# Elementwise sums of a long convolution moved from VectorE to accumulating DMAs inside SBUF

## The chip, the cores and the metric

One core of a Trainium2 chip runs the whole kernel. TensorE (PE) multiplies matrices, ScalarE (ACT) brings its results out of PSUM and computes GELU and scalings, VectorE (DVE) does the elementwise work, GpSimd (POOL) and SyncE (SP) mostly issue DMAs. The metric is the device time of one execution in microseconds (us).

## The reference, cut to what matters

Two branches over the same input `x` (`A_q`, 2048 rows of 640) are mixed by a gate per row. Branch A is a short convolution, a product and a long convolution done by a Fourier transform; branch B is a mixer with two LayerNorms and an MLP.

```python
# A: short convolution of k with 4 taps, times v, then a long causal convolution
for t in range(ks):
    k_shift = k_shift + k_pad[:, t:t + S, :] * shift_k[:, ks - 1 - t][None, None, :]
kv = k_shift * v
y_f = rfft(pad(kv)) * rfft(pad(ssm_k))            # over 2*S points, per column
y = irfft(y_f)[:S] + kv * ssm_D
a = q * y
# B: mixer and MLP
h = gelu(layernorm(x) @ w1)                       # 640 -> 640
x1 = x + concat(four shifted quarters of h) @ w2
b = x1 + gelu(layernorm(x1) @ w3) @ w4            # 640 -> 1536 -> 640
out = g * a + (1 - g) * b                         # g = sigmoid((x * gate_w).sum(-1))
```

The order of the sums in the complex product and in the short convolution is free.

## The kernel before, in words

All data stay in one SBUF tensor, `arena`, 128 partitions wide; every tile is a stretch of it. So the profile names nearly every operand `arena`, and a helper's line stands for many operations: L453 is `tt`, every tensor-tensor operation of DVE; L480 is `evict`, every move from PSUM by ACT; L465 is `act`, ACT on SBUF data; L487 is `load`.

**Order of the work.** The kernel is first written down as a list of nodes in program order. Reads and writes are tracked in pieces of 32 bytes of a partition, and each node depends on the earlier nodes that touch its pieces. `schedule` (L140) then walks through time with an estimated cost for each node and gives every engine a fixed order: the node that can start first goes first, and among equals the one whose tag has the higher number in `PRIO` (L967). A tag is the operation's name and its stage, such as `pw:1`. The engines then run their lists in order, and wait on semaphores for what they need from others. A DMA is modelled as a queue common to all, 390 KB per us, plus 2 us.

**Branch B** runs in groups of rows. First LayerNorm (`ln_bn`, L632, statistics on DVE, the power on POOL at L646, normalization on ACT), transposes on PE (L620), the product with w1 (L715, 100 matmuls), GELU, small moves of the shifted tail from POOL's queue (L743), the product with w2 (L760, L762), second LayerNorm, then w3 (L792) and w4 (L808, L810). The tiles of w3 lie over w1 and w2, those of w4 over `kacc` and `ktmp`, so these loads wait until the earlier users are done. Q, the input once more for the end, lies over the transposed tile and is loaded after the last L792.

**Branch A** has these parts.
- The short convolution, tag `kv`, stages 0 to 3 (block c of 1024 rows, half h of it), L555 to L568: per stage four products of 2560 elements a partition, three sums into `kacc`, one product with v. All stages share one `kacc` and two `ktmp`.
- The long convolution splits the frequencies in two (`kap`) and the columns in two (`half`), so there are four units, run by `conv_unit` (L912) with stage 2*half + kap. Each unit has: `forward` (L834, PE at L844, 32 matmuls, once for the filter, tag `fwdh`, once for kv, `fwdk`), a `window` on the latter (2 operations of 1280), a `butterfly` on each (`bh`, `bk`; 2 operations of 2560, 4 of 1280), `pointwise` (L871, the complex products, 6 of 2560 and 8 of 1280) and `fold` (8 of 1280). The butterflies, the products and the fold all use the slot s4 as a temporary tile, so they follow one another.
- `inverse` (L923, PE at L934, 8 groups of 8 matmuls per half) brings two units back; its results are scaled by ACT (`gy`), multiplied by Q and added on DVE (`fin`), and stored.

At the end of the program `inverse` of the second half needs the fold of the fourth unit.

Of the kernel before, what the change touches and what calls it, by code (L numbers as in the profile page):

```python
# [10 lines left out]
ACTF = mybir.ActivationFunctionType  # L11
ALU = mybir.AluOpType
# [66 lines left out]
class Prog:  # L79
# [48 lines left out]
        job.pe = node  # L128
        return job

    def dma(self, queue, fn, r=(), w=(), nbytes=0, cost=0.1, kind="dma", group=None, final=False, tag=""):
        node = self._new(queue, [fn], cost, kind, r, w, group, tag)
        node.bytes = nbytes
        node.final = final
        return node

    RATE = 390e3
# [203 lines left out]
def bass_gated_mix__ssm_conv_h3__mixer_s_mlp__prompt_kernel(  # L341
# [5 lines left out]
    P = Prog(nc)  # L347
# [17 lines left out]
    def V(o, n):  # L365
        return AR[:, o:o + n]
# [31 lines left out]
    w1t = V(oW12 + 3200, 640).rearrange("p (c f) -> p c f", c=5)  # L398
# [3 lines left out]
    FM = V(oFM, 4096).rearrange("p (a r s i k) -> p a r s i k", a=2, r=4, s=2, i=2)  # L402
    GM = V(oGM, 4096).rearrange("p (a i r s k) -> p a i r s k", a=2, i=2, r=4, s=2)
    TAP = V(oTAP, 10240).rearrange("p (h t d) -> p h t d", h=2, t=16)
    KV = V(oKV, 10240).rearrange("p (t d) -> p t d", t=16)
    slots = {f"s{i}": oS + i * SLOT for i in range(5)}
# [3 lines left out]
    kacc = V(oW4, 2560).rearrange("p (r d) -> p r d", r=4)  # L410
# [41 lines left out]
    def tt(o, a, b, op, n, tag="", **kw):  # L452
        return dve(lambda e: e.tensor_tensor(o, a, b, op), [a, b], [o], n, tag=tag, **kw)  # L453
# [101 lines left out]
    for c in range(2):  # L555
        for h in range(2):
            P.stage = 2 * c + h
            for j in range(4):
                src = KH[c][:, 3 + 4 * h - j:7 + 4 * h - j, :]
                sb = SHK[:, j, :].unsqueeze(1).to_broadcast([128, 4, 640])  # L560
                if j == 0:
                    tt(kacc, src, sb, ALU.mult, 2560, tag="kv")
                else:
                    t = ktmp[j % 2]
                    tt(t, src, sb, ALU.mult, 2560, tag="kv")
                    tt(kacc, kacc, t, ALU.add, 2560, tag="kv")
            o = KV[:, 8 * c + 4 * h:8 * c + 4 * h + 4, :]
            tt(o, kacc, o, ALU.mult, 2560, tag="kv")  # L568

# [255 lines left out]
    def cplx(slot):  # L825

        if slot in ("k0", "k1"):
            return KV[:, :, 320 * int(slot[1]):320 * int(slot[1]) + 320]
        return V(slots[slot], SLOT).rearrange("p (n d) -> p n d", n=16)
# [35 lines left out]
    def window(slot, kap):  # L865
# [2 lines left out]
        tt(S[:, :, 0, 1, :], S[:, :, 0, 1, :], S[:, :, 1, 0, :], a, 1280, tag="win")  # L868
        tt(S[:, :, 1, 1, :], S[:, :, 1, 1, :], S[:, :, 0, 0, :], b, 1280, tag="win")

    def pointwise(sh, sk, sz, temp):  # L871
        H, K, Z = [cplx(s).rearrange("p (i m b) d -> p i m b d", i=2, m=4) for s in (sh, sk, sz)]
        T2 = [V(slots[temp] + 2560 * i, 2560).rearrange("p (m b d) -> p m b d", m=4, b=2) for i in range(2)]
        T1 = [V(slots[temp] + 1280 * i, 1280).rearrange("p (m d) -> p m d", m=4) for i in range(4)]

        def hb(i):
            return H[:, i, :, 0, :].unsqueeze(2).to_broadcast([128, 4, 2, 320])

        tt(Z[:, 0], K[:, 0], hb(0), ALU.mult, 2560, tag="pw")
        tt(T2[0], K[:, 1], hb(1), ALU.mult, 2560, tag="pw")  # L880
        tt(Z[:, 1], K[:, 1], hb(0), ALU.mult, 2560, tag="pw")
        tt(Z[:, 0], Z[:, 0], T2[0], ALU.subtract, 2560, tag="pw")
        tt(T2[1], K[:, 0], hb(1), ALU.mult, 2560, tag="pw")
        h1 = [H[:, i, :, 1, :] for i in range(2)]
        k0 = [K[:, i, :, 0, :] for i in range(2)]
        z1 = [Z[:, i, :, 1, :] for i in range(2)]
        tt(T1[0], k0[0], h1[0], ALU.mult, 1280, tag="pw")
        tt(T1[1], k0[1], h1[1], ALU.mult, 1280, tag="pw")
        tt(Z[:, 1], Z[:, 1], T2[1], ALU.add, 2560, tag="pw")
        tt(z1[0], z1[0], T1[0], ALU.add, 1280, tag="pw")  # L890
        tt(T1[2], k0[1], h1[0], ALU.mult, 1280, tag="pw")
        tt(z1[0], z1[0], T1[1], ALU.subtract, 1280, tag="pw")
        tt(T1[3], k0[0], h1[1], ALU.mult, 1280, tag="pw")
        tt(z1[1], z1[1], T1[2], ALU.add, 1280, tag="pw")
        tt(z1[1], z1[1], T1[3], ALU.add, 1280, tag="pw")
# [16 lines left out]
    def conv_unit(half, kap, A, B, C, T):  # L912
        P.stage = 2 * half + kap
        butterfly(A, T, "bh")
        forward("k", half, kap, B)
        window(B, kap)
        butterfly(B, T, "bk")
        pointwise(A, B, C, T)
        fold(C, T)

    gy_i = [0]
# [1 line left out]
    def inverse(half, slot0, slot1):  # L923
# [41 lines left out]
    inverse(1, "s3", "k0")  # L965

    P.PRIO = {  # L967
        "Sk:2": 147, "xn:4": 146, "fwdk:0": 145, "gelu1t:1": 144, "kv:2": 143, "B:1": 142, "B:0": 141,
        "bn:3": 140, "sq:6": 139, "bn:2": 138, "gelu3:0": 137, "w1t": 136, "mm1:0": 135, "ln:2": 134, "shk": 133,
        "B:3": 132, "warm": 131, "ln:6": 130, "xTp:3": 129, "inv:0": 128, "gate": 127, "bk:2": 126, "kv:3": 125,  # L970
        "tail:0": 124, "gy:0": 123, "Sh:1": 122, "tail:2": 121, "mm2:6": 120, "w2": 119, "xT:6": 118,
        "out:0": 117, "xT:4": 116, "xn:0": 115, "": 114, "w4": 113, "gelu1:3": 112, "gelu1:2": 111, "bk:1": 110,
        "x1:4": 109, "kh": 108, "fin:0": 107, "xTp:0": 106, "fold:1": 105, "tail:3": 104, "pw:3": 103,
        "bn:0": 102, "xn:3": 101, "win:1": 100, "fwdk:2": 99, "fold:2": 98, "bh:0": 97, "ln:4": 96, "mm4:3": 95,
        "mm2:4": 94, "kv:0": 93, "gelu3:2": 92, "q": 91, "Sk:1": 90, "xTe:3": 89, "B:2": 88, "gy:1": 87,
        "x1:6": 86, "pw:2": 85, "tap": 84, "mm4:2": 83, "xT:7": 82, "fwdh:3": 81, "bh:1": 80, "mm4:1": 79,
        "gelu1:1": 78, "fold:0": 77, "fold:3": 76, "mm1:3": 75, "pw:1": 74, "GM": 73, "mm3:0": 72, "Sh:0": 71,
        "x1:7": 70, "xn:1": 69, "drow": 68, "fwdh:1": 67, "x": 66, "Sh:2": 65, "out:1": 64, "mm1:2": 63,
        "fwdk:1": 62, "ln:3": 61, "gelu1:0": 60, "Sk:0": 59, "bk:0": 58, "xn:6": 57, "xTe:1": 56, "xTp:2": 55,
        "w1": 54, "k": 53, "Sk:3": 52, "fin:1": 51, "xT:5": 50, "win:3": 49, "kv:1": 48, "Sh:3": 47, "gw": 46,  # L980
        "ident": 45, "xTp:1": 44, "bh:2": 43, "fwdh:2": 42, "gsum": 41, "tail:1": 40, "xn:7": 39, "mm3:1": 38,
        "xTe:2": 37, "mm1:1": 36, "ln:0": 35, "pw:0": 34, "sq:7": 33, "v": 32, "gelu1t:0": 31, "xn:2": 30,
        "fwdh:0": 29, "w2t": 28, "ssm": 27, "ln:7": 26, "bn:1": 25, "bn:4": 24, "fwdk:3": 23, "inv:1": 22,
        "mm3:2": 21, "xTe:0": 20, "bn:5": 19, "gelu1t:2": 18, "ssmD": 17, "ln:5": 16, "mm3:3": 15, "x1:5": 14,
        "gelu3:3": 13, "w3": 12, "mm2:5": 11, "gelu3:1": 10, "win:2": 9, "bk:3": 8, "win:0": 7, "xn:5": 6,
        "ln:1": 5, "gelu1t:3": 4, "mm4:0": 4, "mm2:7": 3, "bh:3": 2, "FM": 1,
    }
    P.schedule()
    P.assign_waits()
# [30 lines left out]
```

## Time and profile before

| | us |
|---|---|
| median of 3 runs | 256.15 (254.56 to 256.36) |
| profiled execution | 255.79 |
| its span, first to last instruction | 253.7 |
| PE busy (1585 matmuls) | 227.5 |
| DVE busy (323 instructions) | 221.8 |
| ACT busy (244 instructions) | 166.9 |
| POOL busy (43 instructions) | 31.2 |
| granted TensorE clock, mean | 0.99 |

The span begins with the loads: the 16 DMA engines are busy through the first seven of the 40 slices, and move 27.81 MB in all. PE's matmuls are pipelined, so its busy time counts overlaps. One instruction of DVE begins some 0.07 us before the last one ends, so that a row of 1.485 us takes about 1.42 from start to start. In the instruction lists several instructions of one line are merged, and the first one's shape is printed for all.

### The profile page before, as it was taken

The numbers are of one execution on the slowest core, as the hardware profiler recorded it, in microseconds if no ns is written. First come the engines' busy times: TensorE is split into PE (matmuls) and PEld (weight loads), VectorE is DVE, ScalarE is ACT, GpSimd is POOL, SyncE is SP. The second block draws the span as 40 slices with busy tenths as digits, with TensorE's granted clock in tenths as the row PEclk, the third lists the DMA queues.
The fourth block names the chain that finished last, engine by engine and source line by source line (L and its number), as shares of the span: only waits on it lengthen the run. The fifth ranks groups of instructions, "written<-read, shape, count | busy, mean of one in ns | idle before, by whom it ended". The sixth has DMA issues, their size and how long they took to land.

```text
span 253.7 us, 3951 instructions
## 1 busy us (share of the span) xinstructions
PE 227.5 (90%) x1585; PEld 144.7 (57%) x1585; DVE 221.8 (87%) x323; ACT 166.9 (66%) x244; POOL 31.2 (12%) x43
## 2 busy tenths in 40 slices
PE   3037799999999999989999999999999999899992
PEld 1033446956677777634675476677545774377771
DVE  3959999999997999999299999999999999919084
ACT  6085899988699979954888867721744214417283
POOL 6114513006132030202100000000000000000000
PEclk9999999799999999999999999999999999999998
DMA  7999996001057003630056600000000000194034
GB/s 226 225 377 412 411 372 260 3 0 30 16 186 292 0 3 78 199 141 0 0 54 129 126 3 4 0 3 0 0 0 3 0 0 3 21 386 138 27 103 155
DMA packets 21666, 27.81 MB, mean 110 GB/s; under 512 B 12001, under 2 KB 17377, under 8 KB 21393
## 3 DMA queue, kind: packets, MB, share of 16 engines
q1 hardware_dynamic: 19520, 20.55, 25.6%
q0 software_dynamic: 1840, 5.71, 7.1%
q10 hardware_dynamic: 288, 1.31, 1.7%
q8 instruction: 12, 0.20, 0.3%
q14 instruction: 6, 0.04, 0.1%
HBM read 21.79 MB, written 2.62 MB: 96 GB/s over the span
## 4 chain that ended last, share of the span: by engine, by line
PE 80%; DMA 8%; ACT 8%; SPq 2%; issue 1%; DVE 0%; ACTq 0%
PE PS L808 21%; PE PS L792 20%; PE PS L844 12%; PE PS L760 9%; DMA arena<-in_B_w_dram 8%; PE PS L934 7%; PE PS L715 5%; ACT arena L480 5%; ACT arena L465 3%; SPq L487 2%; PE PS L578 2%; PE PS L762 2%; PE PS L810 2%; PE PS L673 1%; DVE arena L453 0%
## 5 line engine op out<-in xcount | busy, mean ns | idle before, releaser
L453 DVE TENSOR_TENSOR arena<-arena 128x1280 bf16<-128x1280 bf16 (+2 forms) x208 | 195.8, 999 | 19.9 <-ACT arena L480 12.8
L480 ACT ACTIVATE arena<-PS 128x640 bf16<-128x640 f32 (+3 forms) x129 | 96.4, 828 | 35.4 <-PE PS L792 24.2
L808 PE MATMUL PS<-arena 128*128 128x320 bf16 x384 | 56.7, 299 | 1.1 <-ACT arena L480 1.1
L792 PE MATMUL PS<-arena 128*128 128x512 bf16 x240 | 52.8, 379 | 1.8 <-DMA arena<-in_B_w_dram 1.8
L480 ACT ACTIVATE arena<-PS,arena 128x320 bf16<-128x320 f32 (+1 forms) x48 | 27.8, 613 | 39.2 <-PE PS L810 36.5
L808 PEld LDWEIGHTS PS<-arena 128*128 128x128 bf16 x384 | 37.4, 98 | 16.6 <-ACT arena L480 1.6
L792 PEld LDWEIGHTS PS<-arena 128*128 128x128 bf16 x240 | 23.4, 98 | 29.4 <-issue 2.1
L465 ACT ACTIVATE arena<-arena 128x640 bf16<-128x640 bf16 (+2 forms) x42 | 33.9, 853 | 6.6 <-DVE arena L647 5.8
L844 PE MATMUL PS<-arena 128*128 128x320 bf16 x256 | 36.2, 299 | 0.0
L844 PEld LDWEIGHTS PS<-arena 128*128 128x128 bf16 x256 | 25.0, 98 | 10.4
L715 PE MATMUL PS<-arena 128*128 128x512 bf16 x100 | 24.3, 396 | 5.7 <-DMA arena<-in_B_w_dram 3.2
L760 PE MATMUL PS<-arena 128*128 128x320 bf16 x160 | 26.2, 299 | 0.1
L640 DVE BATCH_NORM_STATS2 arena<-arena 128x6 f32<-128x320 bf16 x48 | 20.6, 471 | 3.2 <-DMA arena<-in_A_q_dram 3.1
L715 PEld LDWEIGHTS PS<-arena 128*128 128x128 bf16 x100 | 9.7, 101 | 17.7 <-DMA arena<-in_B_w_dram 3.5
L760 PEld LDWEIGHTS PS<-arena 128*128 128x128 bf16 x160 | 15.6, 98 | 6.3 <-issue 0.4
L934 PE MATMUL PS<-arena 128*128 128x320 bf16 x128 | 17.9, 299 | 0.0
L934 PEld LDWEIGHTS PS<-arena 128*128 128x128 bf16 x128 | 12.5, 98 | 5.0
L646 POOL TENSOR_TENSOR arena<-arena 128x4 f32<-128x4 f32 x6 | 9.4, 1566 | 32.3 <-DVE arena L645 32.3
L743 POOL DMA_DIRECT2D arena<-arena x18 | 9.5, 536 | 27.7 <-ACT arena L480 27.7
L620 PE MATMUL PS<-arena 128*128 128x128 bf16 x80 | 6.6, 242 | 4.5 <-ACT arena L465 4.5
L810 PE MATMUL PS<-arena 128*128 128x320 bf16 x32 | 9.6, 299 | 0.0
L762 PE MATMUL PS<-arena 128*128 128x320 bf16 x32 | 9.6, 299 | 0.0
(46 smaller groups left out, 71.3 us busy)
## 6 DMA issues: line engine op xcount, KB each, us to landing
arena<-in_A_q_dram SPq DMA_DIRECT2D x6, 640.0 KB, 7.1
arena<-in_B_w_dram POOLq DMA_DIRECT2D x4, 960.0 KB, 7.0
arena<-in_A_k_dram SPq DMA_DIRECT2D x4, 640.0 KB, 14.5
arena<-in_A_v_dram SPq DMA_DIRECT2D x4, 640.0 KB, 15.1
arena<-in_A_ssm_k_dram SPq DMA_DIRECT2D x5, 512.0 KB, 18.9
out_dram<-arena SPq DMA_DIRECT2D x16, 160.0 KB, 2.0
arena<-in_A_q_dram ACTq DMA_DIRECT2D x2, 640.0 KB, 5.6
arena<-cF SPq DMA_DIRECT2D x1, 1024.0 KB, 20.9
```

The lines of the kernel that those rows point to most:

```text
L453: return dve(lambda e: e.tensor_tensor(o, a, b, op), [a, b], [o], n, tag=tag, **kw)
L465: node = P.op("act", lambda e, ps: e.activation(o, i, func, **kw), r=r, w=[o], cost=c_act(n, naps, acc is not None), tag=tag, group=group)
L480: node = P.op("act", lambda e, ps: e.activation(ov, inner(ps), func, **kw), r=r, w=[o], cost=c_act(n, len(r), acc is not None), job=job, t ...
L640: dve(lambda e, o=o, x=x: e.bn_stats(o, x), [x], [o], 640, tag="bn", group=("bn", g, i))
L715: fns.append(lambda e, ps, b=b, c=c, lhsT=lhsT, sc=sc: e.matmul(bank(ps, b, 512), lhsT, XT[:, c, 2 * sc:2 * sc + 2, :], start=(c == 0), st ...
L760: fns.append(lambda e, ps, hh=hh, ft=ft, lhsT=lhsT: e.matmul(bank(ps, hh, 320), lhsT, w2v[:, ft, 320 * hh:320 * hh + 320], start=(ft == 0) ...
L762: fns.append(lambda e, ps, hh=hh, c=c, rho=rho: e.matmul(bank(ps, hh, 320), ident, X[:, c, rho, 320 * hh:320 * hh + 320], start=False, sto ...
L792: fns.append(lambda e, ps, b=b, ft=ft, c=c, sc=sc: e.matmul(bank(ps, b, 512), w3v[:, c, 128 * ft:128 * ft + 128], XT[:, c, 2 * sc:2 * sc + ...
L808: fns.append(lambda e, ps, hh=hh, ft=ft, lhsT=lhsT: e.matmul(bank(ps, hh, 320), lhsT, w4v[:, ft, 320 * hh:320 * hh + 320], start=(ft == 0) ...
L810: fns.append(lambda e, ps, hh=hh, c=c, rho=rho: e.matmul(bank(ps, hh, 320), ident, X[:, c, rho, 320 * hh:320 * hh + 320], start=False, sto ...
L844: fns.append(lambda e, ps, r=r, ri=ri, s=s, b=b, rhs=rhs: e.matmul(bank(ps, b, 320), FM[:, kap, r, s, ri, :], rhs, start=(s == 0), stop=(s ...
L934: fns.append(lambda e, ps, kap=kap, ri=ri, c=c, r=r, s=s, n=n: e.matmul(bank(ps, c, 320), GM[:, kap, ri, r, s, :], Qs[kap][:, r, ri, c, :] ...
```

## The change

- In the stages 2 and 3 of the short convolution (the second block), each of the three sums into `kacc` is a DMA that POOL issues, from `ktmp` into `kacc`, with addition at the destination. The first block keeps DVE's sums.
- In the units 0, 1 and 2, `pointwise_dma` takes the place of `pointwise`. It has 4 products of 2560 and 4 of 1280 on DVE, most of them written over one of their operands, a negation of 2560 elements on ACT, and six accumulating DMAs: two of 1280 elements a partition into the temporary tile (`pwa`), two of 2560 into the result (`pwb`), two of 1280 from the temporary tile into half of the result (`pwc`). Unit 3 keeps `pointwise`.
- In the planner's terms each such DMA holds POOL for 0.9 us and moves twice its bytes.
- Every number of `PRIO` is another, so the order on every engine and queue may be another too. Some of the new numbers, loads on SP: x 146, w1 128, k 105, v 85, w2 73 (before: x 66, w1 54, k 53, v 32, w2 119).

```diff
@@ kv @@
                     t = ktmp[j % 2]
                     tt(t, src, sb, ALU.mult, 2560, tag="kv")
-                    tt(kacc, kacc, t, ALU.add, 2560, tag="kv")
+                    if c == 0:
+                        tt(kacc, kacc, t, ALU.add, 2560, tag="kv")
+                    else:
+                        o, i = [a.rearrange("p (x r) d -> p x (r d)", x=2) for a in (kacc, t)]
+                        P.dma("pool", lambda e, ps, o=o, i=i: e.dma_start(o, i, accum_op=ALU.add, max_dma_last_dim=2560), r=[o, i], w=[o],
+                              nbytes=2 * 256 * 2560, cost=0.9, tag="kva")
...
+    def accumulate(o, i, n, tag):
+
+        P.dma("pool", lambda e, ps: e.dma_start(o, i, accum_op=ALU.add, max_dma_last_dim=2560), r=[o, i], w=[o], nbytes=2 * 256 * n, cost=0.9,
+              tag=tag)
+
+    def pointwise_dma(sh, sk, sz, temp):
+
+        H, K, Z = [cplx(s).rearrange("p (i m b) d -> p i m b d", i=2, m=4) for s in (sh, sk, sz)]
+        T1 = [V(slots[temp] + 1280 * i, 1280).rearrange("p (m d) -> p m d", m=4) for i in range(2)]
+        h1 = [H[:, i, :, 1, :] for i in range(2)]
+        k0 = [K[:, i, :, 0, :] for i in range(2)]
+        z1 = [Z[:, i, :, 1, :] for i in range(2)]
...
+        tt(T1[0], k0[0], h1[1], ALU.mult, 1280, tag="pw")
+        tt(T1[1], k0[0], h1[0], ALU.mult, 1280, tag="pw")
+        tt(Z[:, 0], K[:, 0], hb(0), ALU.mult, 2560, tag="pw")
+        tt(K[:, 0], K[:, 0], hb(1), ALU.mult, 2560, tag="pw")
+        act(H[:, 1], H[:, 1], ACTF.Copy, 2560, scale=-1.0, tag="neg")
+        tt(h1[0], k0[1], h1[0], ALU.mult, 1280, tag="pw")
+        tt(h1[1], k0[1], h1[1], ALU.mult, 1280, tag="pw")
+        accumulate(T1[0], h1[0], 1280, "pwa")
+        accumulate(T1[1], h1[1], 1280, "pwa")
+        tt(Z[:, 1], K[:, 1], hb(0), ALU.mult, 2560, tag="pw")
+        tt(K[:, 1], K[:, 1], hb(1), ALU.mult, 2560, tag="pw")
+        accumulate(rows(Z[:, 1]), rows(K[:, 0]), 2560, "pwb")
+        accumulate(rows(Z[:, 0]), rows(K[:, 1]), 2560, "pwb")
+        accumulate(z1[1], T1[0], 1280, "pwc")
+        accumulate(z1[0], T1[1], 1280, "pwc")
...
-        pointwise(A, B, C, T)
+        (pointwise if (half, kap) == (1, 1) else pointwise_dma)(A, B, C, T)
```

`hb(i)` is H's first half of part i, repeated over two blocks; `rows` is another view of the same bytes.

## The prediction

> **What bounds the kernel now.** I read the 40 slices first, then each engine's instructions in order of time, then the chain that ended last, the shapes of DVE's groups, and the DMA landings. From the slices (one digit is 6.34 us):
>
> ```profile
> PE   3037799999999999989999999999999999899992
> ...
> DVE  3959999999997999999299999999999999919084
> ACT  6085899988699979954888867721744214417283
> ```
>
> PE and DVE are both full from about 45 us on, ACT only up to about 64 us. Which of the two sets the end is seen in the instruction lists (start, length, what, idle before in brackets). PE:
>
> ```profile
> 20.55 6.92 PE L715 MATMUL PS<-arena 128*128 128x512 bf16 x25 [3.22 <-DMA arena<-in_B_w_dram]
> ...
> 77.14 4.51 PE L844 MATMUL PS<-arena 128*128 128x320 bf16 x32
> ...
> 239.80 8.86 PE L934 MATMUL PS<-arena 128*128 128x320 bf16 x64
> ```
>
> and DVE:
>
> ```profile
> 54.53 20.77 DVE L453 TENSOR_TENSOR arena<-arena 128x2560 bf16<-128x2560 bf16 x15
> ...
> 126.85 95.38 DVE L453 TENSOR_TENSOR arena<-arena 128x1280 bf16<-128x1280 bf16 x102 [3.85 <-ACT arena L480]
> 227.76 6.71 DVE L453 TENSOR_TENSOR arena<-arena 128x640 bf16<-128x640 bf16 x15 [5.53 <-DMA arena<-in_A_q_dram]
> ```
>
> DVE's frequency work is over at 126.85 + 95.38 = 222.2. The last inverse transform, which needs it, starts on PE only at 239.8, because PE still has L808 to do. So the convolution chain on DVE has 17.6 us of slack, and **PE is the bound**: the chain of waits is 80% PE, and PE's only idle after 20.5 us is 1.90 + 0.62 + 0.28 (on ACT, before 46 us), 1.81 (w3) and 1.11, 5.7 us in all. DVE time taken away is worth nothing by itself; a DVE chain made longer costs nothing up to 17.6 us and all beyond.
>
> **What is removed.** Rows by shape:
>
> ```profile
> L453 DVE TENSOR_TENSOR arena<-arena 128x2560 bf16<-128x2560 bf16 x72 | 103.9, 1485 | 0.4
> L453 DVE TENSOR_TENSOR arena<-arena 128x1280 bf16<-128x1280 bf16 x104 | 78.9, 819 | 5.9 <-ACT arena L480 5.6
> ```
>
> A pointwise of 6 x 1.485 + 8 x 0.819 = 15.5 becomes 4 x 1.485 + 4 x 0.819 = 9.2 us; three units, 18.7 us. Six kv sums go, 6 x 1.485 = 8.9. DVE loses 27.6 of 221.8 us. In place of it: three ACT negations of 2560. ACT's 1280-wide row is 1.257 and its 640-wide 0.733, so 0.82 ns an element and 2.3 us each (2.0 to 2.5); ACT has room after 100 us (51 of 95 us busy from 127 to 222). And 24 DMAs on POOL's queue: 12 of 655 KB, 12 of 328 KB.
>
> **One accumulating DMA.** No row shows one. The nearest are the moves inside SBUF that POOL issues at L743:
>
> ```profile
> arena<-arena POOLq DMA_DIRECT2D x6, 32.0 KB, 1.8
> ...
> arena<-in_B_w_dram POOLq DMA_DIRECT2D x2, 960.0 KB, 7.0
> ```
>
> (first line: between 45 and 70 us, DMA nearly idle; the same six between 20 and 45 us, DMA full, took 5.4.) The second line is the two w3 loads together; while they moved, slices showed 353 to 435 GB/s, say 380. They hold POOL 0.86 us each against 0.54 at L743, so the fixed part is 1.8 + 0.3 = 2.1 us. On top of it come the bytes at 380 GB/s: if only the addend counts, 1.72 us for 655 KB; if both operands are read over one path, 3.45; if the write shares it as well, 5.17. So d (655 KB) is 3.8, 5.55 or 7.3 us and c (328 KB) 2.95, 3.8 or 4.7. I take between the last two, d = 6.4 and c = 4.25, because half of these DMAs move runs of 640 bytes, and the tail row shows that company triples a landing.
>
> The Trainium skill, "DMA: Bandwidth & Descriptors", section "Anatomy of one DMA", gives 2.0 us plus bytes over 436 GB/s; "Collectives: The Full Stack", section "The bandwidth ceiling", says that an add costs two source reads and nothing more. By both, estimates are 5.0 and 3.5 us, and the forecast's sum would end PE-bound, at the first rival's time. Against the change speaks "SBUF — State Buffer", section "Summary": descriptor generation for POOL's DMAs starves while DVE runs in its 2x mode. The trace disagrees: DVE was busy 5.90 of 6.00 us from 58 to 64 us while the 1.8 us row landed.
>
> **kv, second block.** kacc is one buffer, so the three sums of a stage, and both stages, are serial: kv:2 from 48.1 us in before. A stage is two products, 3d, then one product. With 1.43 us from start to start, the two stages cost 7 products on the path (10 us with semaphores) and 6d, where before they ended at 73.4 (w4's load, which waits for them, goes out at 73.46), 25.3 us. Now 10 + 6 x 6.4 = 48.4. DVE waits there; butterfly bh:0 (5.8 us) moves in, so that is not lost.
>
> **A unit.** Before, a unit is 5.83 + 5.83 (butterflies) + 14.5 + 6.0 (fold) by start-to-start times, with window 1.5. After, 8.66 + a gap G in place of 14.5. The temp slot s4 serves both butterflies, the products and the fold of every unit, so the next butterfly can't fill G. pwb needs the last product, pwc needs pwb, fold needs pwc: G = d + c + 1 (two transfers side by side at each step; the part of the fold that needs only the first pair is taken off). At my values 11.7 us, against 5.8 of DVE saved in the unit.
>
> **The sum.** The head first. w1, x, k and v stand ahead of the four w2 loads on SP's queue now (priorities 128, 146, 105, 85 against 73; w2 was 119, w1 54, x 66). Those are 655 KB, 1.8 us at 370 GB/s, 2.9 at the 225 GB/s of the first 12 us. PE waited 3.2 us for w1 until 20.5; its XT is evicted at 18.6; ACT idles 2.97 us at 18.6 as DVE's LN steps stand behind the late x. I take 3 us earlier (0 to 3.5). So kv:2 starts at 45.1, kv ends at 45.1 + 48.4 = 93.5. Forward, eviction: 5.5 (77.31 to 82.85). Units: window 1.5, bk 5.83, 8.66, G, fold 6.0 = 22 + G; twice 26.3 + G (their windows fit in the gap); the last 32.2: 106.8 + 3 x 11.65 = 141.75. That is 240.75. I add 1 us a unit for the negation (the product h1[1] and the K1 product stand behind it on DVE, PSUM evictions of PE behind it on ACT) and 2 for the second LayerNorm's DVE work (16 x 0.471 + 8 x 0.198 = 9.1 us, most of it in the gaps): 245.75. The inverse can start 2 before that, when r = 0 is folded, 243.8; 8.71 of PE and the 5.0 us from PE's end (248.71) to 253.7 give a span of 257.5. The profiled time was 255.79 for a span of 253.7, so 259.6; the median of the runs shown stands 0.36 above it: **260.0**.
>
> PE meanwhile: mm2, fwdh:1 and fwdk:0 last it until about 92 to 96, when kv ends, so no gap is priced. POOL's queue is in order: w3, w4, GM and the LN powers (1.57 us) queue behind accumulates that wait for DVE; w3 late would be PE idle, in the range only.
>
> **The rivals.**
> 1. *Faster: DMA cheap, PE still the bound.* From 170.4 + 9d + 3c + 5 - 2 at or below 236.8 (PE's old 239.8 less 3), that is 9d + 3c up to 63.4, d about 5.8. Then only the head counts: 253.7 - 3 + 2.1 = 252.8, 253.1 at the median. For it: reading both operands gives 61.4, just inside. Against: my d leaves nothing for two DMAs meeting loads.
> 2. *Cover without gain.* The same, but the head's 3 us don't come: ACT is busy 22.8 of 24 us from 21 to 45 and may bound it. 255 to 257.
> 3. *Slow accumulates.* d = 7.3, c = 4.7: 250.2 + 5 - 2 + 8.7 + 5 = 266.9, 269 in time; with rows of 640 bytes slower still, beyond. Every stall then reaches PE too, since PE, ACT and POOL run in a fixed order.
>
> **How the numbers follow.** Forecast 0.35, rival 1 0.27, rival 2 0.20, rival 3 0.18. The low end 250.5 is rival 1 with two thirds of PE's later waits gone (2.6 us); the high end 269.5 takes in the upper bound of d and leaves out slower DMAs. One per cent, 2.6 us, is about what a measurement can tell: faster (under 253.6) 0.27, slower (over 258.7) 0.49, which is rival 3 and 0.31 of the forecast's spread; within 0.24, rival 2 and the rest of it.
>
> **What would show it.** Landings of the accumulates near 6.4 and 4.25 us; DVE busy about 194 us; DVE gaps near 12 us before three of the four folds; kv's last product near 93; mm1 starting near 18; PE waiting on DVE before the last L934. Wrong if d is under 5.8, if other DVE work fills the gaps, or if the head stays at 20.5.

## The result, and the profile after

The changed kernel takes 287.82 us (median of four runs, 284.29 to 289.98) against 256.25 for the kernel before on the same chip: 1.120 times as long, interval 1.109 to 1.132. The run of 289.98 is of a slower state and is left out of the ratio. The forecast was 260.0 with a range up to 269.5. The sign was right, the size was not. The profiled execution took 284.29 for a span of 282.2.

From the page of the changed kernel, the slices (7.06 us each) and the chain that ended last, by engine and by line:

```profile
PE   3039959988999299979698999999989999995491
...
DVE  4599998446893209932599940299970199999994
...
PEclk9999999999999779999799999999999999999688
...
DVE 36%; DMA 28%; PE 19%; ACT 10%; issue 4%; POOL 1%; ACTq 0%; POOLq 0%; DVEq 0%
DVE arena L454 33%; DMA arena<-arena 24%; PE PS L798 6%; ACT arena L481 6%; ACT arena L466 4%; PE PS L975 4%; DMA arena<-in_A_q_dram 3%; PE PS L850 3%; PE PS L721 3%; DVE arena L646 2%; PE PS L814 2%; POOL arena L879 1%; PE PS L679 1%; PE PS L626 1%; POOL arena L652 1%
```

Before, the chain was 80% PE. Now PE has 19% of it, and DVE and the DMAs have 64%, 24 of it in moves inside SBUF. Counted from 0, DVE has holes at the slices 7 to 9 and 12 to 14 (kv's second block and its end) and around 17, 24 and 30 (the three units). PE has holes too, at 13, 36 and 37, and its granted clock falls there or right after.

PE's instruction list of the changed kernel (start, length, what, idle before in brackets), where it waits longest after the head:

```profile
21.31 3.69 PE L721 MATMUL PS<-arena 128*128 128x512 bf16 x10 [1.42 <-ACT arena L481]
...
98.30 15.50 PE L850 MATMUL PS<-arena 128*128 128x320 bf16 x92 [5.32 <-DVE arena L454]
...
253.51 4.51 PE L975 MATMUL PS<-arena 128*128 128x320 bf16 x32
264.77 11.43 PE L975 MATMUL PS<-arena 128*128 128x320 bf16 x64 [6.75 <-DVE arena L454]
```

The product with w1 starts 0.8 us later than before, not earlier. PE runs out of other work twice: for 5.32 us until the second block of kv is there, and for 6.75 us until the last fold.

DVE's list shows the gaps, here of the units 1 and 2:

```profile
163.78 2.35 DVE L454 TENSOR_TENSOR arena<-arena 128x1280 bf16<-128x1280 bf16 x2 [0.59 <-ACT arena L466]
178.84 0.82 DVE L454 TENSOR_TENSOR arena<-arena 128x1280 bf16<-128x1280 bf16 x1 [12.71 <-DMA arena<-arena]
182.37 27.37 DVE L454 TENSOR_TENSOR arena<-arena 128x1280 bf16<-128x1280 bf16 x29 [2.70 <-DMA arena<-arena]
222.72 0.82 DVE L454 TENSOR_TENSOR arena<-arena 128x1280 bf16<-128x1280 bf16 x1 [12.97 <-DMA arena<-arena]
226.05 52.25 DVE L454 TENSOR_TENSOR arena<-arena 128x1280 bf16<-128x1280 bf16 x73 [2.50 <-DMA arena<-arena]
```

The last products of unit 1 end at 166.13; one operation of the fold can go at 178.84, the others from 182.37. Unit 2 has the same picture from 209.74 to 226.05. The landings behind it, from the page's DMA issues:

```profile
arena<-arena POOLq DMA_DIRECT2D x12, 640.0 KB, 7.0
...
arena<-arena POOLq DMA_DIRECT2D x12, 320.0 KB, 6.4
```

and pieces of the chain in order of time, from the end of kv and the ends of the units 1 and 2 (start, length, what):

```profile
89.49 7.07 DMA arena<-arena
96.66 1.50 DVE arena L454
98.30 4.44 PE PS L850 x16
...
166.54 10.45 DMA arena<-arena
177.70 4.65 DMA arena<-arena
...
210.15 10.59 DMA arena<-arena
221.41 4.61 DMA arena<-arena
```

One sum of 640 KB with no other sum beside it (kva, at 89.49) takes 7.07, the six of them 5.6 to 7.1 with a median of 6.4, as forecast. The second `pwb` of a unit, of the same size, takes 8.5 in unit 0 and 10.5 and 10.6 in the units 1 and 2. It isn't alone: POOL's list of unit 1 (issues only),

```profile
159.96 1.32 POOL L879 DMA_DIRECT2D arena<-arena  x1 [5.36 <-DVE arena L454]
162.75 1.18 POOL L879 DMA_DIRECT2D arena<-arena  x1 [1.47 <-DVE arena L454]
164.91 1.28 POOL L879 DMA_DIRECT2D arena<-arena  x1 [0.98 <-DVE arena L454]
166.54 1.20 POOL L879 DMA_DIRECT2D arena<-arena  x1 [0.34 <-DVE arena L454]
171.16 1.31 POOL L879 DMA_DIRECT2D arena<-arena  x1 [3.42 <-DMA arena<-arena]
177.70 1.28 POOL L879 DMA_DIRECT2D arena<-arena  x1 [5.24 <-DMA arena<-arena]
```

is one `pwa`, one `pwb`, the other `pwa`, the other `pwb` and the two `pwc`. They land after 5.8, 7.6, 7.6, 10.5, 7.7 and 4.6 us. So while the second `pwb` is under way (166.54 to 177.0), the first one flies until 170.4, the second `pwa` until 172.5 and the first `pwc` from 171.2. Only the last sum of the unit is alone again, and takes 4.6.

### The profile page after: what moved, and what is told of

Same layout as the page of the kernel before. It is cut to its first block, busy times and chain, and to the rows that moved or that the text cites. A ratio compares the mean times of both kernels' runs of the same rounds, so it can differ in the third digit from the quotient of the medians.

```text
span 282.2 us, 3966 instructions
## 1 busy us (share of the span) xinstructions
PE 235.3 (83%) x1585; PEld 143.1 (51%) x1585; DVE 195.9 (69%) x299; ACT 173.1 (61%) x247; POOL 60.8 (22%) x67
## 3 DMA queue, kind: packets, MB, share of 16 engines
HBM read 21.79 MB, written 2.62 MB: 87 GB/s over the span
## 4 chain that ended last, share of the span: by engine, by line
DVE 36%; DMA 28%; PE 19%; ACT 10%; issue 4%; POOL 1%; ACTq 0%; POOLq 0%; DVEq 0%
DVE arena L454 33%; DMA arena<-arena 24%; PE PS L798 6%; ACT arena L481 6%; ACT arena L466 4%; PE PS L975 4%; DMA arena<-in_A_q_dram 3%; PE PS L850 3%; PE PS L721 3%; DVE arena L646 2%; PE PS L814 2%; POOL arena L879 1%; PE PS L679 1%; PE PS L626 1%; POOL arena L652 1%
## 5 line engine op out<-in xcount | busy, mean ns | idle before, releaser
L454 DVE TENSOR_TENSOR arena<-arena 128x1280 bf16<-128x1280 bf16 (+2 forms) x184 | 170.0, 980 | 60.4 <-DMA arena<-arena 41.0
L481 ACT ACTIVATE arena<-PS,arena 128x320 bf16<-128x320 f32 (+1 forms) x48 | 27.8, 616 | 50.7 <-PE PS L816 38.8
L798 PE MATMUL PS<-arena 128*128 128x512 bf16 x240 | 54.8, 387 | 3.8 <-DMA arena<-arena 2.9
L814 PE MATMUL PS<-arena 128*128 128x320 bf16 x384 | 56.6, 299 | 1.2 <-ACT arena L481 1.2
L466 ACT ACTIVATE arena<-arena 128x640 bf16<-128x640 bf16 (+3 forms) x45 | 40.8, 957 | 13.4 <-DVE arena L454 5.2
L850 PE MATMUL PS<-arena 128*128 128x320 bf16 x256 | 39.9, 311 | 7.1 <-DVE arena L454 5.3
L879 POOL DMA_DIRECT2D arena<-arena x18 | 23.4, 1301 | 78.9 <-DVE arena L454 53.4
L766 PE MATMUL PS<-arena 128*128 128x320 bf16 x160 | 26.2, 299 | 2.0 <-DMA arena<-arena 2.0
L975 PE MATMUL PS<-arena 128*128 128x320 bf16 x128 | 20.6, 324 | 6.8 <-DVE arena L454 6.8
L721 PE MATMUL PS<-arena 128*128 128x512 bf16 x100 | 24.1, 396 | 2.4 <-ACT arena L481 2.4
L652 POOL TENSOR_TENSOR arena<-arena 128x4 f32<-128x4 f32 x6 | 8.6, 1433 | 21.6 <-DVE arena L651 18.7
L749 POOL DMA_DIRECT2D arena<-arena x18 | 10.1, 660 | 13.0 <-ACT arena L481 13.0
L571 POOL DMA_DIRECT2D arena<-arena x6 | 7.3, 1224 | 24.4 <-DMA arena<-arena 12.6
```

The costliest lines, as they stand in the source:

```text
L466: node = P.op("act", lambda e, ps: e.activation(o, i, func, **kw), r=r, w=[o], cost=c_act(n, naps, acc is not None), tag=tag, group=group)
L481: node = P.op("act", lambda e, ps: e.activation(ov, inner(ps), func, **kw), r=r, w=[o], cost=c_act(n, len(r), acc is not None), job=job, t ...
L652: P.op("pool", lambda e, ps: e.tensor_tensor(RS, VAR, HALF, ALU.pow), r=[VAR, HALF], w=[RS], cost=1.6, tag="ln")
L721: fns.append(lambda e, ps, b=b, c=c, lhsT=lhsT, sc=sc: e.matmul(bank(ps, b, 512), lhsT, XT[:, c, 2 * sc:2 * sc + 2, :], start=(c == 0), st ...
L766: fns.append(lambda e, ps, hh=hh, ft=ft, lhsT=lhsT: e.matmul(bank(ps, hh, 320), lhsT, w2v[:, ft, 320 * hh:320 * hh + 320], start=(ft == 0) ...
L798: fns.append(lambda e, ps, b=b, ft=ft, c=c, sc=sc: e.matmul(bank(ps, b, 512), w3v[:, c, 128 * ft:128 * ft + 128], XT[:, c, 2 * sc:2 * sc + ...
```

## The experiments

Theory after the first look: the bytes of the accumulates set the time, by holding up kv's second block and by gaps of 13 to 16 us in three units. Rivals: the new order alone is to blame; the fixed part of a DMA is; moving the bytes is, whether they are added or not; the planner believed the DMAs too cheap.

### The parts, with the planner choosing a new order

Sums on DVE again, with the new `PRIO` (e_order); only kv's sums by DMA (e_kv); only the products' (e_pw); no sums at all (e_none).

```diff
-                    if c == 0:
+                    if True:
                         tt(kacc, kacc, t, ALU.add, 2560, tag="kv")
...
-        (pointwise if (half, kap) == (1, 1) else pointwise_dma)(A, B, C, T)
+        pointwise(A, B, C, T)
```

Both edits are e_order, the second alone is e_kv, the first alone e_pw. In e_none `accumulate` and the accumulates of kv are taken out.

> All sums back on DVE as in the kernel before; only the new priority numbers, so the new order, stay. If the accumulating DMAs are the cause, this is a DVE chain that again ends with slack, and PE bounds: 253 to 259 us, DVE busy about 222. If the new order is the cause, most of the 31 us stays: over 275.

> Only kv's second block sums by DMA; pointwise as before. The chain theory: in the changed kernel the six serial landings (6.5 us each) make these two stages take 46 + 3 us from kv:2's first product, 25.3 before, so the chain is 22 to 24 us longer and spends the 17.6 us of slack: 258 to 264 us. If the loss sat in the products' sums alone: 253 to 257. If kv's part carried it all: over 275.

> Only the sums of three units' products by DMA; kv as before. The chain theory: a gap of 15 us (measured in the changed kernel) in place of 5.8 us of DVE work in each unit, 9 to 10 us a unit, 28 in all, less 17.6 of slack: 264 to 270 us. If kv's wait alone is the cause: 253 to 257. If the parts simply add up without slack in common: about 275.

> The 24 accumulating DMAs are left out and nothing takes their place, so the sums are missing from the result; products, negations and order rules stay. It shows what the idea is worth if the sums were free. PE-bound theory: DVE's 27.6 us are worth nothing but PE's stalls, 251 to 256 us. If DVE time were worth something by itself: under 245. If the order or the negations on ACT are the cause: over 270.

Measured, as ratios to the kernel before on the same chip: e_order 266.24 us (1.042, 1.038 to 1.046), e_kv 274.33 (1.076, 1.073 to 1.078), e_pw 322.69 (1.264, 1.261 to 1.267), e_none 268.83 (1.052, 1.049 to 1.056). None is where a theory put it, and e_none, which does less than e_order, is no faster. In all four the planner has drawn up another order, since it works on another list of nodes with the same numbers. In e_pw the order is so unlucky that PE stands idle for 51.81 us before the last inverse:

```profile
303.84 11.77 PE L975 MATMUL PS<-arena 128*128 128x320 bf16 x64 [51.81 <-DVE arena L454]
```

So these runs tell only one thing safely: without any accumulating DMA, an order drawn up with this `PRIO` still costs some 11 us (e_order). What a part costs can't be read from them; the order has to be held.

### The DMAs made small, or turned into copies

e_small sends only 64 elements a partition in each of the 24 DMAs; e_copy sends all bytes but doesn't add. Nodes and costs are the planner's same ones, and in e_copy every engine has the order of the changed kernel. In e_small it hasn't: the smaller DMAs touch fewer pieces, so the planner sees fewer dependencies, and from about 113 us on PE, ACT and DVE have a somewhat different order (PE, for one, 64 matmuls of `forward` in a row where the changed kernel has 32, then 10 of w3, then 32).

```diff
+        o, i = o[:, 0:1, 0:64], i[:, 0:1, 0:64]
```

(e_small, ahead of both kinds of DMA)

```diff
-        P.dma("pool", lambda e, ps: e.dma_start(o, i, accum_op=ALU.add, max_dma_last_dim=2560), r=[o, i], w=[o], nbytes=2 * 256 * n, cost=0.9,
+        P.dma("pool", lambda e, ps: e.dma_start(o, i, max_dma_last_dim=2560), r=[o, i], w=[o], nbytes=2 * 256 * n, cost=0.9,
```

(e_copy, likewise in kv)

> Every accumulating DMA stays with its waits but adds only the first 64 elements of each partition (16 KB instead of 655 or 328 KB), so most of each sum is left out of the result. If bytes make the landing long (7.0 and 6.4 us median in the changed kernel), it falls to 2 to 3 us, the chain is some 40 us shorter and PE bounds: 253 to 258 us. If the fixed part of such a DMA (issue 1.3 us, waits, POOL's order) makes it long, landings stay over 4 us and the time over 265.

> The same 24 DMAs with the same bytes, as plain copies: the sums are left out of the result, the addend overwrites the destination. If the second read of an add is what takes the time, 655 KB land in 2.1 + 1.7 to 3.5 = 4 to 5.5 us and the time falls to 256 to 268. If moving the bytes inside SBUF from POOL's queue is the price, add or not, landings stay at 6 to 7 us and the time over 278.

Measured: e_small 260.87 (1.020, 1.015 to 1.026), e_copy 264.73 (1.036, 1.031 to 1.040). In e_copy the landings are

```profile
arena<-arena POOLq DMA_DIRECT2D x12, 640.0 KB, 4.1
arena<-arena POOLq DMA_DIRECT2D x12, 320.0 KB, 3.6
```

and DVE's gap in unit 1 is half as long (its products end at 157.66):

```profile
164.87 0.82 DVE L454 TENSOR_TENSOR arena<-arena 128x1280 bf16<-128x1280 bf16 x1 [7.20 <-DMA arena<-arena]
165.85 25.11 DVE L454 TENSOR_TENSOR arena<-arena 128x1280 bf16<-128x1280 bf16 x27 [0.16 <-DMA arena<-arena]
```

In this unit the six land after 4.2, 3.8, 3.3, 4.1, 5.9 and 3.2 us, the second `pwb` after 4.1 where the sum needs 10.5. **The same bytes moved without adding cost 23 us less.** (Adding also cuts them into more packets: for one unit 2656 against 672. Whether a part of the 23 is due to that, no run separates.) The other 9 of the 32 us by which the changed kernel is slower are there with copies too; e_small, in its own order, has about 5.

How the 19.8 us between the spans of e_copy (262.4) and the changed kernel (282.2) reach PE is read from the two lists: in e_copy the last inverse, then 96 matmuls in a row, starts without a wait at 243.23,

```profile
243.23 13.20 PE L975 MATMUL PS<-arena 128*128 128x320 bf16 x96
```

in the changed kernel its first 32 matmuls start at 253.51. So 10.3 us arise in the middle, 6.75 as the wait before the last 64, and these take 11.43 for 8.8.

### Each half of the bytes

s_kv cuts only the products' DMAs to 64 elements a partition, s_pw only those of kv; the edit is the line of e_small at one place. s_pw has the changed kernel's order on every engine; s_kv, which its expectation says has it too, has the order of e_small.

> The changed kernel in exactly its order on every engine; kv's six accumulating DMAs whole, the 18 of the products with only the first 64 elements of each partition, so most of those sums is left out. With all 24 cut the time was 260.9, with none 287.8. Chain theory: the two parts share one slack; kv's bytes are worth 6 x 4.2 = 25 us on the chain and most of it goes into the slack: 262 to 270. If the parts add up without a slack: about 274. If kv's part is the cause alone: 283 to 288.

> As before in exactly the changed kernel's order, the 18 DMAs of the products whole, kv's six cut to 64 elements (most of those sums left out). Chain theory: three gaps of 15 us fall to some 6 when cut, so 27 us on the chain, most in the shared slack: 262 to 272. Additive without slack: about 274. If the products' part is the cause alone: 283 to 288.

Measured: s_kv 269.98 (1.057, 1.052 to 1.061), s_pw 278.02 (1.090, 1.086 to 1.095): 9.1 and 17.1 above e_small. kv's bytes can be priced twice, each time in one order: 9.1 us without the products' bytes (s_kv less e_small) and 9.8 with them (287.82 less s_pw). If the two parts shared a slack, the first would be smaller by it. So they share none to speak of, though s_kv's time alone lies inside the range that was expected from a shared one. The products' part, 17 to 18 us, was only measured together with the difference between the two orders. PE in s_kv, then in s_pw:

```profile
100.15 15.67 PE L850 MATMUL PS<-arena 128*128 128x320 bf16 x92 [5.05 <-DVE arena L454]
```

```profile
259.36 10.36 PE L976 MATMUL PS<-arena 128*128 128x320 bf16 x64 [7.75 <-DVE arena L454]
```

kv's lateness is paid at 100 us: PE has nothing else in its order then, and what is lost there is lost for good, though DVE still has slack at the end (in s_kv the last inverse starts at 247.52 without a wait). The products' lateness is paid partly in the units and partly before the last inverse.

### The order alone

p_dve keeps the exact order of the changed kernel, written out as a list, and puts a DVE sum where each DMA stood.

```diff
-    P.schedule()
+    P.replay(SEQ, PAIR)
```

> The changed kernel's order kept on every engine, but each of the 24 sums is a DVE operation at the place in the order where POOL issued the DMA; negations on ACT and products stay. If the DMAs' landings are the cause and the order in itself is sound, PE bounds again: 254 to 262 us. If the order is a cause of its own, it stays over 266 as with the new priorities and the old sums (266.2).

Measured: 265.04 (1.037, 1.033 to 1.041), between the two expectations and equal to e_copy. Sums on DVE in this order cost as much as copies by DMA. e_small stands 4.2 below; most of the difference is a fall of TensorE's clock near 40 us that the traces of p_dve and e_copy show and e_small's doesn't. The line of the clock on the pages of e_small and of p_dve (e_copy's reads like p_dve's), one fence each:

```profile
PEclk9999999999999999999999999999999999999998
```

```profile
PEclk9999995799999999999999999999999999999998
```

The product with w2 starts at 58.85 in e_small, at 62.35 in e_copy and 62.06 in p_dve. So the changed kernel's order costs 9 to 10 us with this fall; less the 3.2 to 3.5 us of it, some 6 are left, which is an estimate.

### The head

b_w2p holds the order of the kernel before and moves only w2's four loads, on SP's queue, from ahead of the others to behind the last of `ssm`; it tests the forecast's 3 us. b_ln, b_kh and b_khln hold the order of before as well: in b_ln the small steps of the first LayerNorm group go ahead of the second group's statistics; in b_kh the loads of `kh` go behind w1, with w2 first as before; b_khln is both. In each the edit is the list's.

> The kernel before with its order kept on every engine; only on SP's queue the four w2 loads (655 KB) are issued after the ssm loads and not ahead of kh, x and w1. The prediction's term for the head by itself: w1 and the second half of x land 1.8 to 2.9 us earlier, PE is bound from there on: 253 to 254.5 us against 256. If PE's start is set by something else (XT evicted at 18.6, LN steps on DVE, ACT): 255.5 to 257.

> The kernel before, order kept, but the small LayerNorm operations of group 1 stand on DVE ahead of group 2's statistics, which wait for the second half of x. ACT's wait of 2.97 us at 18.6 us should go. If ACT bounds the head (busy 22.8 of 24 us after it): 252.5 to 254.5. If PE's wait for w1 (until 20.5) bounds it: 255 to 256.5.

> The kernel before, order kept, but SP issues the halo loads kh (0.96 MB) after w1 and not ahead of x and w1; the w2 loads stay first. If what lands beside x's first half decides the head (in the new order, x's second half beside it, PE's first transposes came 2.6 us later; with kh beside it 2.0 later), then x's second half beside the end of the first half costs some of what w1's earlier landing gives: 254 to 257. If w1's landing alone decides: 252.5 to 254.

> Both of the last two edits. If the head is bound by ACT's start on group 1 and by w1 together, only this one gains all of it: 251.5 to 253.5. If x's first half lands later for it, no gain: 255 to 257.

Measured: b_w2p 257.12 (1.006, 1.004 to 1.009), b_ln 254.96 (0.9995, 0.9976 to 1.0015), b_kh 254.19 (0.998, 0.996 to 1.000), b_khln 254.08 (0.995, 0.993 to 0.997). In b_w2p w1 is early and PE's wait for it is gone, but the first transposes start later, since the first half of x, loaded over ACT's queue, lands later. The DMA issues of b_w2p and its PE list:

```profile
arena<-in_A_q_dram ACTq DMA_DIRECT2D x2, 640.0 KB, 6.5
```

```profile
16.55 1.23 PE L644 MATMUL PS<-arena 128*128 128x128 bf16 x10 [6.90 <-ACT arena L489]
...
20.75 3.57 PE L739 MATMUL PS<-arena 128*128 128x512 bf16 x8 [1.42 <-ACT arena L504]
```

Before, x landed in 5.6 us and the transposes started at 14.55. The forecast gained w1 and lost x. b_kh gets both, by putting large loads behind w1 and leaving w2 in front:

```profile
14.68 1.23 PE L644 MATMUL PS<-arena 128*128 128x128 bf16 x10 [5.24 <-ACT arena L489]
...
18.88 5.47 PE L739 MATMUL PS<-arena 128*128 128x512 bf16 x17 [1.42 <-ACT arena L504]
```

Here the product with w1 starts 1.67 us earlier than before, but the time isn't clear of noise. b_khln's is: it beats both kernels, by half a per cent against the one before.

### Filling the gaps, and telling the planner the true price

e_bh gives `bh` another temporary tile, so that it could run in the gap, and lets the planner order anew; e_plan tells the planner three times the bytes in place of two; p_bh holds the changed kernel's order, gives `bh` of the units 2 and 3 a slot that is free then, and moves it right behind the last product of the unit before.

```diff
-        butterfly(A, T, "bh")
+        butterfly(A, T if (half, kap) == (0, 0) else B, "bh")
```

```diff
-                              nbytes=2 * 256 * 2560, cost=0.9, tag="kva")
+                              nbytes=3 * 256 * 2560, cost=0.9, tag="kva")
```

```diff
-        butterfly(A, T, "bh")
+        butterfly(A, {2: "s2", 3: "t0"}.get(2 * half + kap, T), "bh")
```

(e_bh, e_plan and p_bh)

> The changed kernel, but the filter's butterfly of units 1 to 3 uses as its temporary tile the slot that the unit's forward transform fills later, and not s4; so it can run in the gap that the accumulating DMAs of the unit before leave. If the shared slot is why the gap is not filled, 5.8 us come back per gap: three gaps, 15 to 18 us, 270 to 274 us. If the gap is kept open by something else (DMAs that read that slot, POOL's order), 282 to 290.

> The changed kernel with the planner told three times the bytes of each accumulating DMA instead of twice, that is 7.0 and 4.5 us to landing, near the measured ones for a single DMA; only the order of the engines changes. If the landings on one chain are the cause, the order helps little: 280 to 288 us. If engines stalled in a wrong order (PE, ACT, POOL waiting at an instruction while others were ready) are the cause: under 268.

> The changed kernel with its order kept, but the filter's butterflies of units 2 and 3 use a free slot as temporary tile (the slot of the filter of the unit before, or of unit 2) and stand in DVE's order right after the last product of the unit before, so that they run while the accumulating DMAs land. If the gaps are open only because all share s4, two gaps of 15 us take 5.8 us of work each: 11 us off the chain, 275 to 279 us. If a gap must stay empty (DVE disturbs the landings, or other waits take over): 283 or more.

Measured: e_bh 341.87 (1.333, 1.324 to 1.342), e_plan 344.10 (1.347, 1.341 to 1.353), p_bh 284.13 (1.115, 1.110 to 1.119). The first two again have other orders in which the last inverse stands 62.22 and 68.48 us; that of e_plan:

```profile
326.49 10.81 PE L975 MATMUL PS<-arena 128*128 128x320 bf16 x64 [68.48 <-DVE arena L454]
```

So a truer price alone, with numbers in `PRIO` that were found for the other one, makes the order worse; this says nothing of what a new search would give. p_bh is the clean one. Its DVE, ACT and PE lists, one fence each:

```profile
172.33 4.56 DVE L478 TENSOR_TENSOR arena<-arena 128x2560 bf16<-128x2560 bf16 x5 [5.06 <-DMA arena<-arena]
```

```profile
175.45 2.49 ACT L505 ACTIVATE arena<-PS 128x640 bf16<-128x640 f32 x4 [7.93 <-DVE arena L478]
```

```profile
176.21 4.45 PE L822 MATMUL PS<-arena 128*128 128x512 bf16 x10 [7.35 <-ACT arena L505]
...
262.29 13.20 PE L999 MATMUL PS<-arena 128*128 128x320 bf16 x96
```

DVE works in the gap, its last fold ends at 249.9, where the changed kernel has the first half of it only at 264.7, and the last inverse waits no more. The gain is still at most 3.7 us, and hardly clear of noise: the changed kernel's repeats further down took 285.23 and 287.89. The reason is that the borrowed slot is one that ACT fills next: ACT's eviction into it waits 7.93 us and PE behind it 7.35. The wait has moved from the end to the middle.

### What makes the second sum slow

Two more runs asked whether the length of the rows or the addition itself makes the second `pwb` slow (the expectations call the two `pwb` of a unit a pair). r_long writes `pwb` of the units 0 and 1 with rows of 2560 bytes, r_short writes kv's sums with rows of 640.

```diff
-            return a.rearrange("p m b d -> p (m b) d")
+            if sk[0] == "k":
+                return a.rearrange("p m b d -> p (m b) d")
+            return a.rearrange("p (x m) b d -> p x (m b d)", x=2)
```

```diff
-                        o, i = [a.rearrange("p (x r) d -> p x (r d)", x=2) for a in (kacc, t)]
+                        o, i = [a.rearrange("p r (y d) -> p (r y) d", y=2) for a in (kacc, t)]
```

> The changed kernel with the same order and bytes; only the two sums of 2560 elements a partition in the units 0 and 1 (pwb) are written as 2 rows of 2560 bytes a partition in place of 8 rows of 640. In the changed kernel's trace the sum into kacc, written in rows of 2560 bytes, was 272 packets and kept 16 engines busy 63.8% of 5.7 us, 0.214 us a packet; stretches with rows of 640 bytes alone had 619 packets in 67.2% of 4.6 us, 0.080 us a packet. Theory A, a packet has a fixed part of its own: the pair of sums falls from 2048 packets to 512, from some 164 us of engine time to 110, so the second of the pair lands after 7 to 8 us in place of 10.5; the gaps of the units 0 and 1 lose about 3 us each, and the time falls by 4 to 6 us against 287.8, to 282 to 284. Unit 2, unchanged, keeps 10.5. Theory B, only the bytes added count: packets may change, landings and time don't, 287 to 288.

> The changed kernel with the same order and bytes; only the six sums into kacc (kva) are written as 8 rows of 640 bytes a partition in place of 2 rows of 2560. Theory A, a packet has a fixed part of its own: 1024 packets of 0.080 us in place of 256 of 0.214, 82 us of engine time in place of 55, 1.7 us more on each landing (6.4 to about 8), all six on the path: the second block of kv ends some 9 us later and the time is 294 to 298. Theory B, only the bytes added count: landings stay near 6.4 us, the time stays at 287 to 288.

Measured: 285.23 (1.118, 1.113 to 1.124) and 287.89 (1.124, 1.116 to 1.132). The premise was wrong: the same row stands on the page of all three kernels,

```profile
DMA packets 32802, 39.61 MB, mean 139 GB/s; under 512 B 12384, under 2 KB 25952, under 8 KB 32528
```

(this one is r_long's; the changed kernel's differs in the mean alone, 140). Whatever way the rows are written, the packets are the same, so the edits changed nothing, and the two runs are repeats of the changed kernel. The question has part of an answer all the same, in the changed kernel's own trace. A sum of kv alone is 272 packets (65.86 to 71.50). Unit 2 has an operand that lies in rows of 640 bytes, unit 1 has none for `pwb`. So POOL's queue has 2656 packets in the window of unit 1 (159.9 to 182.4) and 4192 in that of unit 2 (203.6 to 226.1), for the same 2.62 MB; the difference is what two `pwb` of 1040 packets in place of 272 come to, an estimate. The second `pwb` lands after 10.45 in unit 1 and 10.59 in unit 2. So it needs no more packets than a sum of kv to be 4 us slower; what it has is company. That packets cost nothing isn't shown: in unit 1 transposes on SP's queue took another 14.7% of the engines' time, in unit 2 nothing did, and in unit 0, with 2656 packets as well, the second `pwb` took only 8.5.

## Why the prediction was wrong, step by step

The terms of the sum against the profiled execution:

| step | forecast | measured | difference |
|---|---|---|---|
| first DMA of kv's second block issued | 48.0 | 51.72 | +3.7 |
| from there to the end of its last product | 45.5 | 46.4 | +0.9 |
| forward transform and eviction | 5.5 | 7.7 | +2.2 |
| three gaps G | 35.0 | 13.5 + 15.5 + 15.6 | +9.6 |
| the rest of the three units | | | +1.2 |
| the last unit, to the start of the inverse | 30.2 | 33.5 | +3.3 |
| last inverse on PE | 8.7 | 11.4 | +2.7 |
| from PE's end to the span's end | 5.0 | 6.0 | +1.0 |
| median against the profiled execution | 0.4 | 3.5 | +3.2 |

Together 27.8 us, which is 287.82 - 260.0. A gap is taken from the end of the last product to the end of the fold, less the fold's 6.0; the forecast for the first row is 45.1 plus the two products ahead of the DMA.

- **"PE is the bound, DVE's chain has 17.6 us of slack"** was right for the kernel before, and used wrongly. The slack at the end was counted as if any delay on the way could draw on it. s_kv shows that it can't: PE's order has a place, at 95 us there and at 93 in the changed kernel, where all that is left needs kv.
- **"d = 6.4, c = 4.25"**: right for sums that have no other sum beside them (median 6.4 for the six of kv; the last `pwc` of a unit 4.6 to 4.9). Of the two reasons for going above 5.55, kv's sums don't have the rows of 640 bytes; company they have, of moves and transposes: the only one with nothing else moving (65.86 to 71.50) took 5.64, next to the 5.55 of both operands read over one path. The 5.0 and 3.5 that were estimated from the pages are low.
- **"G = d + c + 1, two transfers side by side at each step"** failed, and is the largest term. It let sums run side by side at the price of one. In unit 1: 0.4 from the last product to the issue of the second `pwb`, 10.45 and 0.7 until the last `pwc` is issued, 4.65 for that one, less 0.75 for the one operation of the fold that could go before: 15.5 where the forecast had 11.65. The forecast reckoned with company from loads, never with that of the sums for each other.
- **"PE lasts until 92 to 96, when kv ends, so no gap is priced"** failed by a little, and cost more than the little. PE ran out at 92.97; kv ended at 98.15. The 5.32 us of idle time came with a granted clock of 0.58 from 95 to 100 us and 0.74 from 100 to 105: the first 16 matmuls took 4.44 us, where 16 of the same kind take 2.34 at 166.78. That is the +2.2 of the forward transform. An estimate with no margin should have carried a price.
- **"3 us earlier at the head"** had the wrong sign: the product with w1 came 0.8 later than before, and with the steps behind it the row is +3.7. It priced the load that comes sooner and not the one that it pushes back: b_w2p.
- **The new order at nothing.** Apart from the head, the forecast took the order as neutral. p_dve and e_copy put it at 9 to 10 us with the fall of the clock, some 6 without. The +3.3 of the last unit is of this kind: final operations of the first half (`fin`, 8 of them with 3.3 us of DVE) stand between its steps. So rival 1, DMAs cheap enough for PE to stay the bound, would not have given 253.1 in an order like this, but something near e_small's 260.9.
- **What was right**: the chain kv, units, last fold with the gaps where they were forecast; the negation (2.33 us, forecast 2.3); DVE busy 195.9 (forecast 194); PE waiting for DVE before the last inverse; rival 3 as the side on which it would go wrong, and its remark that every stall then reaches PE, though the sums were slow in company and not, as rival 3 has it, each by itself.

## What to carry to other kernels

Price a DMA that stands on a chain with the others that fly at the same moment, and an addition inside a DMA at more than a copy; what is free on an idle queue is not free as a link between two operations of a full engine. Slack that shows at the end of a kernel covers nothing that stalls an in-order engine in its middle, so look for the last place at which that engine has other work. When a kernel's order comes from numbers tuned for one list of nodes, hold the order while testing a part, or the test measures the order; and look whether it was held, since an edit that only makes a transfer smaller takes dependencies out as well (e_small).

## What the runs showed of the hardware

- An accumulating DMA of 640 KB inside SBUF landed in 5.6 to 7.1 us with no other sum beside it, in up to 10.6 with others; as a copy in 3.5 to 5.8, with a median of 4.1. With 64 elements a partition it landed in 2.2. With nothing else moving, a sum took 5.64 (at 65.86) and a copy 3.53 (at 55.37 in e_copy); less the 2.2 that is 2.6 times as long. The 16 DMA engines were busy for 64.5% of the 5.64 us and for 47.3% of the 3.53, 2.2 times as long. The Trainium skill, "Collectives: The Full Stack", section "The bandwidth ceiling", says, of reductions between ranks, that an add costs two source reads; the engines' busy time here is near that, the landing less its fixed part is above it. What sums do to each other is seen in unit 2 (203.6 to 226.1 us), when nothing else moved: POOL's queue kept the 16 DMA engines 95.9% busy for 2.62 MB, a mean of 117 GB/s; with loads, slices showed up to 409. That the sums share the engines' reads is a reading of these numbers; no run separated it.
- Other DMAs are late beside sums as well. The 16 transposes on SP's queue landed after a median of 2.7 us before and in e_small, after 4.1 in e_copy and 5.8 in the changed kernel, where PE waited 2.94 us for one, until 136.64.
- POOL was held 1.2 to 1.3 us by the issue of a sum (twice 1.56), 0.7 to 0.8 by that of a copy of the same tiles (once 0.90).
- In these traces TensorE's granted clock fell to half after idle or thin stretches, and stayed there some us into the work that followed. The changed kernel around the last inverse (us of the window, busy time of each engine, granted clock, DMA share, GB/s):

```profile
258.00:264.70 6.70, 0.02 (x1) 0.00 (x0) 6.63 (x10) 0.95 (x2) 0.00 (x0) 0.88 0.16 49
264.70:267.00 2.30, 2.23 (x8) 1.03 (x8) 2.30 (x5) 0.00 (x0) 0.00 (x0) 0.50 0.00 0
267.00:269.00 2.00, 2.00 (x9) 1.15 (x9) 2.00 (x6) 0.84 (x2) 0.00 (x0) 0.50 0.00 0
269.00:271.00 2.00, 2.00 (x13) 1.27 (x12) 2.00 (x6) 1.19 (x4) 0.00 (x0) 0.78 0.53 164
271.00:273.00 2.00, 2.00 (x17) 1.46 (x15) 1.80 (x5) 1.76 (x4) 0.00 (x0) 1.00 0.69 216
```

  After 6.75 us without a matmul the clock is 0.50 until about 269.9 (0.78 on average from 269 to 271), 5 us into the inverse: that is where 2.7 us went.
- The same fall near 40 us is a matter of the run. In this order PE is busy only 1.1 to 1.6 of the 4 us from 36 to 40. With 1.39 in e_small and 1.46 in the changed kernel's profile the clock stayed at 1.00, with 1.14 in e_copy it was 0.50 from 40 to 48, and with 1.61 in s_pw 0.57 from 40 to 44, so the busy time alone doesn't decide it. Of the four runs of r_short, three had a mean clock of 0.943 or 0.944 and spans of 285.8 to 286.0, one had 0.966 and 282.5. The changed kernel's profiled execution had 0.966 and 282.2, two others 0.954 and 0.955 and 285.3 and 286.1. Those two have no trace, but the repeats r_long and r_short have one each: with the fall the product with w2 starts at 62.83 and 62.43 in place of 59.22, and the last 64 matmuls of the inverse at 268.14 and 268.88 in place of 264.77. So the +3.2 of the table's last row is most likely this fall.
- The first half of x, on ACT's queue, landed in 5.1 to 5.6 us with w2's loads first on SP's queue (before, b_ln, b_kh, b_khln), in 6.5 and 6.7 with other loads ahead of them (b_w2p, the changed kernel). What it is in those loads that makes the difference, no run separates.
